# Seven unread matmuls in two waits of TensorE, ahead of the output stage of a recurrence and soft-MoE kernel

## The chip, the cores and the metric

The kernel runs on one core of one Trainium2 chip. The core has a matrix engine (TensorE, in the profile PE, with its weight loads listed apart as PEld), VectorE (DVE), ScalarE (ACT), GpSimd (POOL) and SyncE (SP), which run their own instruction streams and wait for each other through semaphores, and 16 DMA engines that move data between the chip's memory and the core's buffers (SBUF). Matmul results go to PSUM, which has 8 banks. The metric is the device time of one execution in microseconds, lower is better.

## The reference

Two steps. First a gated recurrence over 4 sequences of 5056 tokens and 256 channels; then a mixture of experts with soft slots over all 20224 tokens, with 8 experts of 4 slots:

```python
f = lower_bound + (1 - lower_bound) * sigmoid(f_logit);  i = 1 - f
for t in range(S):
    h = f[:, t] * h + i[:, t] * x[:, t];  y[:, t] = h
x = y.reshape(B * S, D)                                  # 20224 x 256
logits = x @ phi                                         # 20224 x 32
d = softmax(logits, over tokens);  slot_input = d.T @ x  # 32 x 256
for e in range(8):                                       # 4 slots each, F = 1024
    slot_out[e] = relu(slot_input[e] @ w1[e]) @ w2[e]
out = softmax(logits, over slots) @ slot_out             # 20224 x 256
```

Nothing of the output can be computed before all tokens have been seen, since `slot_input` sums over all of them.

## The kernel before

The work has three stages, and the order of the instructions on each engine is written out by hand.

The first stage (to about 126 us) runs over 40 units of 512 tokens of one sequence: load `f_logit` and `x`, sigmoid on ScalarE, gating on GpSimd, transposes on TensorE, the scan on VectorE, logits and their exponentials. The exponentials stay in SBUF as `etall` (32 slots of each of the 4 sequences on the 128 partitions, 5056 tokens). The expert weights are loaded meanwhile by GpSimd's DMA queue (`load_w`); the last two w2 matrices reuse a tile of the input buffers and appear in the profile as `w_t`.

The second stage (to about 142 us) computes the 32 slot outputs: hidden layer (L619), transposes (L634), the first four experts' second layer (L655), row sums of the exponentials (`row_sums`, L393, with reciprocals on VectorE at L664, L677 and L678), and the last four experts' second layer (L667): for each of them 8 matmuls into the PSUM tile `so_ps`. The last two experts' matmuls wait for `w_t`; the last expert's weights come in three parts. Then VectorE scales the sum to `slot_out` (L680), and GpSimd makes a second form of it, `slot_bd` (L682).

`spin(dst, k, w)` (L150 to L153) issues k matmuls of w columns with expert 0's first weights on both sides; nobody reads what they write. The kernel has three calls of it: 6 of 256 columns each before and after the transformation of the slot inputs, and 8 of 128 columns behind the last L667 matmul.

The third stage writes the output, 20.7 MB, in blocks. `pieces(0, 0)` does the first 2048 tokens of sequence 0: 16 matmuls of 256 columns (L699) into eight PSUM tiles, scaled by VectorE (L689) and ScalarE (L693) in turn, and seven output DMAs (L721). Then come `couple(end, 0)` and `couple(end, 1)`, `rest()`, `whole(0, 1)` and the other couples: matmuls of 512 columns for two sequences at once (L749), scaled by VectorE (L754) and ScalarE (L760), two DMAs each (L763). All output DMAs are issued by SyncE. The PSUM tiles of the couples take the banks that `pieces` used, so TensorE's stream holds a separate wait instruction ahead of the first L749 matmul, until VectorE has read the last of `pieces`. A second such wait stands ahead of the first L667 matmul.

On the chip a matmul of bf16 values is two TensorE instructions, a weight load and the matmul. In the numbering of the change's description, the first output matmul (L699) is TensorE's instruction 2217; the wait ahead of the first L667 is then 2083, and the wait ahead of the first L749 is 2248.

Of the kernel before, what the change touches and what calls it, by code (L numbers as in the profile page):

```python
# [9 lines left out]
F32 = mybir.dt.float32  # L10
# [8 lines left out]
def kernel(  # L19
# [11 lines left out]
    B, S, D = x.shape  # L31
# [4 lines left out]
    P = 128  # L36
# [113 lines left out]
    def spin(dst, k, w):  # L150
        for _ in range(k):
            nc.tensor.matmul(dst[:, ds(0, w)], w1_sb[0][:, 0, :P], w1_sb[0][:, 0, :w],
                             start=True, stop=True, skip_group_check=True)  # L153
# [8 lines left out]
    with tc.tile_pool(name="sp2", bufs=3) as sp2, \  # L162
# [225 lines left out]
        def row_sums(i):  # L388

            t0, n_r = blocks[i]  # L390
            ew = etall[:, ds(t0, P * n_r)].rearrange("s (p r) -> s p r", r=n_r)
            for r in range(n_r):
                nc.tensor.matmul(sums[:, ds((t0 // P + r) * B, P)], ew[:, :, r], ones,  # L393
                                 start=True, stop=True, skip_group_check=True)
            if i == len(blocks) - 1:
                nc.tensor.matmul(rs_ps[:, n_grp * R - 1, ds(0, B // 2)],
                                 left.rearrange("s t u -> s (t u)"), pair_ones,
                                 start=True, stop=True, skip_group_check=True)
# [196 lines left out]
    with tc.tile_pool(name="ew", bufs=1) as ew, \  # L595
         tc.tile_pool(name="pm", bufs=2, space=PSUM) as pm, \
         tc.tile_pool(name="pbig", bufs=1, space=PSUM) as pbig:

        rep2 = rep.rearrange("p b s -> p (b s)")

        sin = ew.tile([P, DC, NS], BF16, name="sin")
        nc.vector.tensor_scalar_mul(sin[:, 0], sin_ps[:, 0], omlb[:, ds(0, 1)])
        nc.scalar.activation(sin[:, 1], sin_ps[:, 1], ACT.Copy, scale=omlb[:, ds(1, 1)])

        cs1 = ew.tile([P, 1], F32, name="cs1")
        nc.vector.tensor_reduce(cs1, csum, AX.X, ALU.add)


        Q = 4
        H = F // 2  # L610
        his = []
        for q in range(E // Q):
            hi = ew.tile([P, F], BF16, name=f"hi{q}")
            for k in range(2):
                hi_ps = (psu.tile([P, H], F32, name="hi_ps", tag="up") if q == 0 else
                         pbig.tile([P, H], F32, name="hi_ps", tag=f"hi_ps{k}"))
                for o in range(DC):
                    for j in range(Q):
                        nc.tensor.matmul(hi_ps[ds(j * NS, NS)], sin[:, o],  # L619
                                         w1_sb[q * Q + j][:, o, ds(k * H, H)],  # L620
                                         start=(o == 0), stop=(o == DC - 1),
                                         skip_group_check=True)
                if k == 0:
                    nc.scalar.activation(hi[:, ds(k * H, H)], hi_ps, ACT.Relu)
                else:
                    nc.vector.tensor_scalar_max(hi[:, ds(k * H, H)], hi_ps, 0.0)
            his.append(hi)
        cs_ps = pm.tile([P, 1], F32, name="cs_ps", tag="pm")
        rcs = ew.tile([P, 1], F32, name="rcs")
        for q in range(E // Q):  # L630
            ht_ps = psu.tile([P, FC, P], BF16, name="ht_ps", tag="up")
            hi_v = his[q].rearrange("p (c f) -> p f c", f=FC)
            for fc in range(FC):
                nc.tensor.transpose(ht_ps[:, fc], hi_v[:, fc], ident)  # L634
            if q == 0:
                nc.tensor.matmul(cs_ps, rep2, cs1, start=True, stop=True)
                src = ht_ps.rearrange("p f (j s) -> p f j s", s=NS)[:, :, :, ds(0, SPE)]
                src = bass.AP(tensor=src.tensor, offset=src.offset,
                              ap=[list(src.ap[0]), [P, FC], [NS + SPE, Q], [1, SPE]])
                dst = hid[:, :, :, ds(0, SPE)]  # L640
                dst = bass.AP(tensor=dst.tensor, offset=dst.offset,
                              ap=[list(dst.ap[0]), [Q * NS, FC], [NS + SPE, Q], [1, SPE]])
                nc.scalar.copy(dst, src)
                nc.vector.reciprocal(rcs, cs_ps)
                continue
            for j in range(Q):
                s0 = (Q + j) * SPE
                src = ht_ps[:, :, ds(j * NS + s0, SPE)]
                copy = nc.scalar.copy if j % 2 == 0 else nc.vector.tensor_copy
                copy(wide[:, :, j, :, ds(s0, SPE)],  # L650
                     src.unsqueeze(2).broadcast_to([P, FC, B, SPE]))
        so4_ps = pm.tile([P, D], F32, name="so4_ps", tag="pm")
        for e in range(Q):
            for fc in range(FC):
                nc.tensor.matmul(so4_ps[ds(fc % 4 * NS, NS), :], hid[:, fc, e],  # L655
                                 w2_sb[e][:, fc],
                                 start=(e == 0 and fc < 4),
                                 stop=(e == Q - 1 and fc >= FC - 4),
                                 skip_group_check=True)
        so4 = ew.tile([P, D], F32, name="so4")  # L660
        nc.vector.tensor_copy(so4, so4_ps)
        so_ps = pm.tile([P, D], F32, name="so_ps", tag="pm")
        row_sums(0)
        nc.vector.reciprocal(rrow[:, :wide_r], rs_ps[:, :wide_r])  # L664
        for j in range(Q):
            for fc in range(FC):
                nc.tensor.matmul(so_ps, wide[:, fc, j].rearrange("p b s -> p (b s)"),  # L667
                                 w2_sb[Q + j][:, fc], start=j == 0 and fc == 0,
                                 stop=j == Q - 1 and fc == FC - 1, skip_group_check=True)
            if j == 0:  # L670
                nc.tensor.matmul(so_ps, rep2, so4, start=False, stop=False,
                                 skip_group_check=True)
                row_sums(1)
            if j == 1:
                row_sums(2)
                q = n_grp * R - 1
                nc.vector.reciprocal(rrow[:, wide_r:q], rs_ps[:, wide_r:q])  # L677
                nc.vector.reciprocal(rrow[:, q, ds(0, B // 2)], rs_ps[:, q, ds(0, B // 2)])  # L678
        spin(tail[:, 1], 8, P)
        nc.vector.tensor_scalar_mul(slot_out, so_ps, rcs)  # L680
        for u in range(2):
            nc.gpsimd.tensor_scalar_mul(slot_bd[:, u], slot_out, parity[:, ds(u, 1)])  # L682
# [138 lines left out]
```

## Time and profile before

| | us |
|---|---|
| median of 3 runs (199.0 to 199.07) | 199.04 |
| profiled execution, its own time | 198.93 |
| its span, first to last instruction | 197.2 |
| TensorE busy / VectorE / ScalarE / GpSimd | 150.5 / 142.1 / 138.2 / 103.2 |
| last weight part (`w_t`) landed | 142.04 |
| first output matmul (L699) started | 143.04 |
| first couple's matmul (L749) started | 146.42 |
| last L749 matmul ended | 175.55 |

The granted TensorE clock is 0.86 in the mean: 1.00 for most of the time to 145.46 us, 0.50 from there on. The DMA engines moved 70.75 MB in 14161 packets.

Times inside the profile are microseconds from the start of the span. Idle time on an engine that ends nothing costs nothing, so the profile is read from the last event backwards: what did the end wait for, and what did that wait for in turn.

### The profile page before, as it was taken

Reading aid. Unit: us, or ns where it says so; the run is one execution under the profiler, and the core shown is the slowest. Engines: PE = TensorE matmul, PEld = TensorE weight load, DVE = VectorE, ACT = ScalarE, POOL = GpSimd, SP = SyncE. Lnnn points to the kernel's source line nnn. Section 1 sums busy time; section 2 is a strip of 40 time slices with the busy share of each in tenths; the row PEclk is TensorE's granted clock in tenths of the full one; section 3 lists DMA queues with packets and bytes.
Section 4 is the critical chain, followed back from the end, with each engine's and each line's share of the span. In section 5 each row is a group of like instructions: output and inputs, shape, how many; then the busy total and the mean of one; then the engine's idle time right before and its main releaser. Section 6 shows DMA issues by size and latency. Waiting matters only on the chain.

```text
span 197.2 us, 3212 instructions
## 1 busy us (share of the span) xinstructions
PE 150.5 (76%) x1188; PEld 105.2 (53%) x1188; DVE 142.1 (72%) x163; ACT 138.2 (70%) x193; POOL 103.2 (52%) x78
## 2 busy tenths in 40 slices
PE   0688598897999979897988888998669999960000
PEld 0476467675766858665776676667443643410000
DVE  2669779989799999999999999332268878840000
ACT  3588678799799998999898797240058889990000
POOL 2589577874998488894969986290030000000000
PEclk9999789999999999999999999999975555555555
DMA  6999999999999999999999999999658999999995
GB/s 210 418 419 421 430 427 422 425 427 352 384 430 420 391 352 422 430 409 307 407 422 374 257 217 214 214 213 213 117 219 345 422 450 429 422 425 425 429 425 216
DMA packets 14161, 70.75 MB, mean 359 GB/s; under 512 B 1585, under 2 KB 2866, under 8 KB 10178
## 3 DMA queue, kind: packets, MB, share of 16 engines
q1 hardware_dynamic: 11520, 62.13, 76.2%
q0 software_dynamic: 2624, 8.42, 21.4%
q8 instruction: 9, 0.15, 0.3%
q14 instruction: 6, 0.05, 0.1%
q10 hardware_dynamic: 2, 0.00, 0.0%
HBM read 58.23 MB, written 20.71 MB: 400 GB/s over the span
## 4 chain that ended last, share of the span: by engine, by line
DMA 36%; PE 29%; DVE 13%; POOL 4%; issue 4%; ACT 3%; ACTq 0%; SPq 0%; DVEq 0%; POOLq 0%
DMA x_t<-in_x_dram 14%; PE op L749 12%; DVE h L313 9%; DMA w_sb<-in_moe_w_dram 7%; DMA w_t<-in_moe_w_dram 7%; DMA f_t<-in_f_logit_dram 7%; POOL u_t L246 4%; PE hp L326 4%; PE up L267 3%; PE sp L261 3%; DVE ht L345 3%; PE op L699 2%; PE slot_ps L183 1%; PE lg L359 1%; DVE ob L689 1%
## 5 line engine op out<-in xcount | busy, mean ns | idle before, releaser
L246 POOL TENSOR_TENSOR u_t<-s_t,x_t 128x1024 bf16<-128x1024 bf16 (+1 forms) x39 | 82.4, 2128 | 22.1 <-ACT s_t L235 14.3
L313 DVE TENSOR_TENSOR_SCAN h<-a,h,up 128x512 bf16<-128x512 f32 (+1 forms) x72 | 86.8, 1252 | 4.4 <-PE up L267 1.7
L235 ACT ACTIVATE s_t<-f_t 128x2048 bf16<-128x2048 f32 (+2 forms) x23 | 38.3, 1668 | 6.3 <-DMA f_t<-in_f_logit_dram 6.0
L326 PE MATMUL hp<-ident_f,h 128*128 128x128 f32 (+1 forms) x160 | 29.3, 307 | 8.2 <-DVE ht L345 6.4
L326 PEld LDWEIGHTS hp<-ident_f,h 128*128 128x128 f32 (+1 forms) x160 | 23.2, 207 | 19.3 <-DVE ht L345 12.8
L261 PE MATMUL sp<-ident_f,s_t 128*128 128x128 f32 x144 | 22.3, 300 | 6.7 <-ACT s_t L235 4.5
L749 PE MATMUL op<-slot_bd,etall 64*128 64x512 bf16 x62 | 25.0, 621 | 1.6 <-DVE ob L689 1.4
L295 ACT ACTIVATE a<-sp,lbs 128x1024 f32<-128x1024 bf16 x24 | 25.5, 1116 | 0.6 <-PE sp L261 0.6
L760 ACT ACTIVATE oc<-op,rrow 128x256 f32<-128x256 f32 x60 | 22.8, 489 | 3.6 <-PE op L749 3.0
L754 DVE TENSOR_TENSOR oc<-op,rrow 128x1024 f32<-128x1024 f32 x16 | 19.3, 1221 | 6.1 <-PE op L749 6.1
L261 PEld LDWEIGHTS sp<-ident_f,s_t 128*128 128x128 f32 x144 | 18.0, 155 | 8.7 <-ACT s_t L235 5.3
L302 ACT ACTIVATE a<-sp,lbs 128x512 f32<-128x512 bf16 (+2 forms) x22 | 17.8, 858 | 4.7 <-PE sp L261 4.3
L267 PE MATMUL up<-ident_f,u_t 64*128 64x64 f32 x192 | 17.8, 230 | 2.2 <-POOL u_t L246 2.1
L749 PEld LDWEIGHTS <-etall 64*128 64x128 bf16 x62 | 9.0, 155 | 16.2 <-issue 12.5
L267 PEld LDWEIGHTS up<-ident_f,u_t 64*128 64x128 f32 x192 | 14.0, 138 | 6.2 <-POOL u_t L246 2.8
L183 PE MATMUL slot_ps<-rep,ident_f 128*128 128x256 f32 x52 | 16.4, 410 | 0.0
L345 ACT COPY ht<-hp 128x512 f32<-128x512 f32 (+1 forms) x20 | 11.7, 583 | 3.8 <-PE hp L326 3.7
L345 DVE COPY ht<-hp 128x512 f32<-128x512 f32 (+1 forms) x20 | 13.3, 667 | 0.8 <-PE hp L326 0.8
L693 ACT ACTIVATE ob<-op,rrow 128x256 f32<-128x256 f32 x15 | 5.8, 478 | 11.2 <-PE op L699 11.1
L313 DVE TENSOR_TENSOR_SCAN h<-a,up 128x512 bf16<-128x512 f32 x8 | 9.3, 1209 | 2.6 <-ACT a L302 1.7
L261 PE MATMUL up<-ident_f,u_t 128*128 128x128 f32 x48 | 9.4, 327 | 0.7 <-POOL u_t L246 0.7
L359 PE MATMUL lg<-h,phi 128*32 128x512 bf16 (+1 forms) x80 | 9.4, 389 | 0.3 <-ACT et L383 0.2
(109 smaller groups left out, 145.7 us busy)
## 6 DMA issues: line engine op xcount, KB each, us to landing
f_t<-in_f_logit_dram SPq DMA_DIRECT2D x12, 1024.0 KB, 12.3
x_t<-in_x_dram SPq DMA_DIRECT2D x12, 1024.0 KB, 11.5
out_dram<-oc SPq DMA_DIRECT2D x6, 2048.0 KB, 11.3
w_sb<-in_moe_w_dram POOLq DMA_DIRECT2D x14, 512.0 KB, 10.9
f_t<-in_f_logit_dram SPq DMA_DIRECT2D x12, 512.0 KB, 8.5
x_t<-in_x_dram SPq DMA_DIRECT2D x12, 512.0 KB, 9.9
out_dram<-oc SPq DMA_DIRECT2D x4, 896.0 KB, 5.9
out_dram<-ob SPq DMA_DIRECT2D x1, 2048.0 KB, 8.7
```

Source lines behind the costliest of these rows:

```text
L183: nc.tensor.matmul(slot_bank[:, 1], ident_f, wide_rep, start=False, stop=False, skip_group_check=True)
L235: nc.scalar.activation(s_t, f_t, ACT.Sigmoid, scale=-1.0)
L246: nc.gpsimd.tensor_tensor(uts[n][:, :r], s_t[:, :r], x_t[:, :r], ALU.mult)
L261: nc.tensor.transpose(ps[:, :, r], t[:, r], ident_f)
L267: nc.tensor.transpose(v[:, :, r], t(r)[k].bitcast(F32), ident_f[k, k])
L295: nc.scalar.activation(a, sp[:, :, :, :, o], ACT.Identity, scale=nomlb[:, ds(o, 1)], bias=1.0)
L313: nc.vector.tensor_tensor_scan(h[:, :T, o], decays[n // 2, o][:, n % 2, :T], up[:, :T, o], hs[number(g - 1, b)][:, ds(used(g - 1) - 1, 1), ...
L326: nc.tensor.transpose(hp[:n_p, r], hw[:, :n_p, r], ident_f)
L345: copy(hts[g][:n_p, b].rearrange("p r d -> p (r d)").bitcast(F32), hps.pop(n)[:n_p].rearrange("p r c -> p (r c)"))
L749: nc.tensor.matmul(op[:, i_r].rearrange("p u d -> p (u d)"), ew[:, :, r + i_r], slot_bd[ds(j * 2 * NS, 2 * NS)].rearrange("s u d -> s (u d)"),
L754: nc.vector.tensor_tensor(ob[:, :, ds(r, k)].rearrange("p u r d -> p r u d"), op[:, ds(0, k)], scale[:, ds(r, k)].unsqueeze(3).broadcast_t ...
L760: nc.scalar.activation(ob[:, u, r + i_r], op[:, i_r, u], ACT.Copy, scale=scale[:, r + i_r, ds(u, 1)])
```

## The change

Seven calls' worth of matmuls are added to TensorE's stream with the existing `spin`: three of 256 columns behind `row_sums(0)` and ahead of the first L667 matmul, four behind `row_sums(2)`. They write to a tile of their own, `unread`, which has the PSUM bank of an earlier tile (`hi_ps0`), and which nobody reads. Each is a weight load and a matmul, so that all later TensorE instructions have a number higher by 6 behind the first call, and by 14 behind the second. The wait ahead of the first L667 becomes 2089, the first output matmul 2231, and the wait ahead of the first L749 2262. The other engines' instructions and their order are the same, and so are the DMAs; semaphore values that count TensorE's matmuls are higher by up to seven. Lines behind the change move by 2 or 3.

```diff
         row_sums(0)
         nc.vector.reciprocal(rrow[:, :wide_r], rs_ps[:, :wide_r])
+        unread = pbig.tile([P, H], F32, name="unread", tag="hi_ps0")
+        spin(unread, 3, D)
         for j in range(Q):
             for fc in range(FC):
                 nc.tensor.matmul(so_ps, wide[:, fc, j].rearrange("p b s -> p (b s)"),
...
             if j == 1:
                 row_sums(2)
+                spin(unread, 4, D)
                 q = n_grp * R - 1
                 nc.vector.reciprocal(rrow[:, wide_r:q], rs_ps[:, wide_r:q])
```

## The prediction

> **What bounds the kernel now.** I read four views, from the end backwards. First SyncE's own waits, which say what the last instruction waited for:
>
> ```profile
> SPq L763 <- DVE oc L754: 17.8, 5, 4.9
> SPq L816 <- DMA out_dram<-oc: 17.3, 1, 17.3
> ```
>
> Columns: total us, times, longest us. The program ends on the landing of the last output transfer, 17.3 us after everything else of SyncE's. TensorE, VectorE and ScalarE are done at 177 us of 197.2. So what counts is when the 16 DMA engines get through 20.7 MB of output. Second, the chain of waits up to the first output:
>
> ```profile
> 127.48 14.56 DMA w_t<-in_moe_w_dram
> 142.08 0.39 PE so_ps L667 x2
> ...
> 143.46 2.83 DVE ob L689 x5
> 146.42 1.90 PE op L749 x4
> ```
>
> The last expert weights land at 142.04, and the output stage hangs on them. Third, stretches of the output stage (after the start and length come the engines' busy times, then the granted TensorE clock, the DMA engines' mean busy share and GB/s):
>
> ```profile
> 127.00:142.00 15.00, 12.78 (x168) 9.90 (x167) 4.08 (x12) 2.28 (x6) 5.91 (x7) 1.00 1.00 195
> 142.70:144.70 2.00, 1.87 (x19) 1.70 (x17) 1.52 (x4) 1.14 (x4) 1.54 (x2) 1.00 0.03 8
> 145.25:146.00 0.75, 0.00 (x0) 0.00 (x0) 0.75 (x2) 0.75 (x3) 0.00 (x0) 0.64 0.68 242
> 146.00:148.20 2.20, 1.78 (x5) 0.74 (x7) 0.93 (x2) 0.25 (x1) 0.00 (x0) 0.50 1.07 413
> 150.55:151.20 0.65, 0.65 (x3) 0.23 (x2) 0.65 (x1) 0.28 (x2) 0.00 (x0) 0.50 0.06 25
> 152.20:194.70 42.50, 23.34 (x66) 9.64 (x64) 18.99 (x17) 22.95 (x61) 0.00 (x0) 0.50 1.01 428
> ```
>
> The transfers are nearly idle until 144.7, full from 146 to 150.3, and full from 151.35 to the end. Between, at 150.55 to 151.20, the share is 0.06: one engine of sixteen works, fifteen wait for the first couple block. Fourth, the queues:
>
> ```profile
> q1 hardware_dynamic: 11520, 62.13, 76.2%
> q8 instruction: 9, 0.15, 0.3%
> ```
>
> Queue 8 fetched instructions nine times, 16384 B each. The packet records behind this view give the starts: 29.61, 49.45, 62.38, 76.58, 93.30, 107.51, 124.61, 134.88, 148.29 us. Numbered as in the change's words (first output matmul 2217), TensorE had by then started instructions 207, 509, 731, 993, 1259, 1497, 1764, 2087, 2258: on average (2258-207)/8 = 256.4 apart. So a fetch belongs to every 256th TensorE instruction, and the ninth falls into the saturated output stage. It lasts 1.02 us on one DMA engine. The same records show that engine late with the first block's output: its last packet of it ends at 152.16, fourteen others' at 150.3 to 150.5, the last other's at 150.91. The parts: six 2048-byte packets before the fetch took 145 instead of 84 ns (0.37), the fetch 1.02, the next two 441 and 254 instead of 159 (0.38); together 1.77. The idle stretch to 151.35 hides 0.9 of it; the rest stays to the end, where that engine lands last, at 195.49. Another lands at 195.18, the other fourteen at 194.73 to 194.89.
>
> **The change part by part.** The profiled execution took 198.93 us (span 197.2, 1.73 around it), 0.11 under the median of 199.04; gains are worked out inside it and taken off the median.
>
> Three unread matmuls stand behind the first row sums. One of this form starts 0.11 us after the one before (L152, 128x256: six in 0.82 us, 273 ns each). They fill 133.87 to about 134.4, where TensorE stood for 0.69 us until VectorE's reciprocal (L664) let L667 start at 134.73. That reciprocal waits for the row sums' last matmul, ahead of the three. What is left is 0.3 us, and behind it stands the wait for weights at 139.49; cost 0. If that cover were gone: 0.33 us. The first of them waits for an earlier matmul into its PSUM bank, done by 130.4.
>
> Four more stand behind row_sums(2): from 138.39, last end about 139.0. TensorE waited there until 139.49 for w_t, later parts landing up to 142.04; cost 0, or 0.44 with weights over 0.5 us earlier. No other engine's order changes, no DMA is added; semaphore counts only shift by 7.
>
> What moves: each later TensorE instruction has a number 14 higher, so the ninth fetch comes 14 instructions sooner. When, depends on a wait. TensorE's sequencer stops at waits of its own; the one ahead of the first L749 is number 2248, passed at 146.31 (VectorE's last ob), and becomes 2262. The number F that triggers the ninth fetch is bounded so:
> - The fetch came 1.98 us after that wait was passed. If F were 2248 or less, the sequencer could have reached it with the first outputs, 143.0 to 144.4, and the lag would be 3.9 us or more on idle engines. So F is at least 2249, and the lag from trigger to packet at most 1.98.
> - The sixth fetch (107.51) came 1.32 us after wait 1491 (106.19). With a lag over 1.32, its trigger lay at or before 1491, and F, 3x256 later, is at most 2259. The fourth (76.58, wait 985 at 75.41) says 2265 with a lag over 1.17.
> - A lag near 2 also fits the other fetches, with the sequencer some 20 instructions ahead of the matmul running.
>
> So F lies in 2249 to 2259 if the lag is 1.32 to 1.98, and then the wait, now 2262, no longer stands before it: the trigger falls among the first outputs, at 142.5 to 144.4, and the packet at about 144 to 146.4 instead of 148.29.
>
> The Trainium skill (Runtime: NRT & Kernel Launch, Instruction fetch mechanics) says that code comes in 16 KiB blocks of 256 instructions, fits the spacing above, and calls the cost of a boundary mostly hidden. By that rule the change would be worth nothing and the time 199.04; the packet rows show an engine that ends late, so I go by them.
>
> What the move is worth. Below: a fetch at 144.8 or later keeps its 1.77, less what is idle in 145.25 to 146.00 (share 0.68: 0.24). That engine would end the first block at 150.4+1.53 = 151.94 instead of 152.16: gain 0.2. Above: packet done before 144.8, nothing late; the last landing is then 195.18 (gain 0.31) or, if the second engine's delay (28 packets of 615 to 649 instead of 611 ns, between 160 and 180 us) is not there in other executions, 194.87 (gain 0.62). Between: a fetch that costs 0.9 or less in 144.4 to 146 is wholly hidden by the idle 150.4 to 151.35. The likeliest start is near 145, so mostly hidden: I take 0.45, midway between 0.31 and 0.62. Sum: 0 + 0 - 0.45, 199.04 - 0.45 = 198.6. Its own range is gains of 0.2 to 0.65: 198.4 to 198.84.
>
> **Rivals.**
> - *The fetch doesn't move* (the change does not do what its number suggests): the lag is under 1.3 us and F in 2263 to 2273, so that the wait still holds it back; 14 instructions are then at most some 0.3 us. For: engines without load could be quicker. Against: the slowed packets that belong to the fetch begin at 147.4, only 1.1 us after the wait. 199.04, within 0.15.
> - *Slower: the fetch meets the last weights.* If the sequencer looks 60 or more instructions ahead, it triggers while TensorE waits at 139.5 to 140; two us later the packet stands in front of weight packets (their last start at 141.7) on one engine. Price: the eighth fetch took 0.94 us, all of it on the chain into 142.04, so 199.04+0.94 less the 0.6 gained = 199.4. It decides from a trigger before 139.9, where TensorE is at number 2192 of the new count. Against: the ninth fetch's wait at 2248 would not matter then in the way seen, and 20 ahead fits all nine.
> - *The clock holds one window longer.* The granted clock fell from 1.00 to 0.50 at 145.46 in the records; four more matmuls in 138.4 to 139.0 might put that off. The first couple's matmuls (427 ns apart, as against 109 for half the columns at full clock) would come twice as fast, the couple up to 1.0 us sooner, and the idle 150.4 to 151.35 would shrink: 198.0 to 197.8. Against: the stretch in which it fell, 142 to 145.5, is untouched, and the clock was 1.00 all through 127 to 142 without them.
>
> **How the numbers follow.** A measurement tells about 0.2% (0.4 us) from no change. Fetch moves: 0.64, of which 0.44 gain over 0.4 us and 0.20 less. Doesn't move: 0.22, all but 0.04 (split evenly) within the bound. Meets the weights: 0.09, slower. Clock: 0.05, faster. Faster 0.44+0.02+0.05 = 0.51; same 0.20+0.18 = 0.38; slower 0.09+0.02 = 0.11. The range, 198.2 to 199.2, leaves out the clock's case, the weights' and the outer parts of the rest, about 0.16.
>
> **What would show it.** Right: the ninth packet of queue 8 starts before 146.4; no engine works alone in the idle stretch before the couple, and the last landings lie closer together; L667 still starts by its weights at 139.49 and 142.08, the first L699 at 143.04. Wrong: a fetch still at 148, weights landing after 142.1, a clock other than 0.50 from 145.5, or a late engine without a fetch on it, which would mean that I have blamed the wrong cause.

## The result and the profile after

The changed kernel took 198.74 us in the median of 15 runs (197.89 to 198.85), the kernel before 199.04 (198.76 to 199.6, 15 runs): a ratio of 0.997, 95% interval 0.9957 to 0.9982. The forecast was 198.6.

The stretches after, with the columns as before: length, the five engines' busy times, granted TensorE clock, mean busy share of the DMA engines, GB/s.

```profile
127.00:142.00 15.00, 13.67 (x176) 10.48 (x174) 4.17 (x12) 2.28 (x6) 5.90 (x7) 1.00 1.00 196
142.70:144.70 2.00, 1.87 (x20) 1.70 (x18) 1.52 (x4) 1.05 (x3) 1.45 (x2) 1.00 0.06 12
150.75:151.30 0.55, 0.55 (x2) 0.23 (x2) 0.55 (x1) 0.18 (x2) 0.00 (x0) 0.50 0.00 0
152.20:194.70 42.50, 23.41 (x67) 9.72 (x64) 19.08 (x17) 23.00 (x61) 0.00 (x0) 0.50 1.01 430
```

Two rows differ. Between the first block and the first couple the share is 0.00: the engine that worked alone there before (0.06) is done when the others are. And in 142.7 to 144.7, where nearly nothing moved, the share is up from 0.03 to 0.06: the ninth instruction fetch now lies there. The packet records have it at 143.30 instead of 148.29 us, 1.36 us long (a fetch of queue 14 at 144.00 overlaps it). The first block's last packets end at 150.55 to 150.69 on all sixteen engines, as against 152.16 on the late engine before.

The two waits of TensorE, with the new matmuls in them (start, length, what; in brackets the idle time left and what ended it):

```profile
133.97 0.49 PE L152 MATMUL unread<-w_sb 128*128 128x256 bf16 x3
134.81 1.03 PE L669 MATMUL so_ps<-w_sb,wide 128*128 128x256 bf16 x8 [0.35 <-DVE rrow L664]
...
138.44 0.60 PE L152 MATMUL unread<-w_sb 128*128 128x256 bf16 x4
139.57 0.60 PE L669 MATMUL so_ps<-w_t,wide 128*128 128x256 bf16 x4 [0.53 <-DMA w_t<-in_moe_w_dram]
```

Both waits are still ended by what ended them before. The end hangs on the same thing, too:

```profile
SPq L819 <- DMA out_dram<-oc: 17.1, 1, 17.1
SPq L766 <- DVE oc L757: 3.6, 1, 3.6
```

To compare executions whose first stages differ by some tenths, the table takes the time from the start of the first output matmul to the end of the last output packet (last column but one), with the start of the fetch (the ninth; in `e5_late` the tenth) and the moment from which the granted clock is 0.50. The rows below the second are the experiments that follow; each is one profiled execution. The last column is that execution's own time.

| run | first output no. | wait no. | first output, us | fetch, us | clock 0.50 from | to last packet | us |
|---|---|---|---|---|---|---|---|
| before | 2217 | 2248 | 143.04 | 148.29 | 145.46 | 52.45 | 198.93 |
| the change | 2231 | 2262 | 143.12 | 143.30 | 146.14 | 52.13 | 198.84 |
| before_again | 2217 | 2248 | 143.21 | 144.13 | 147.77 | 51.86 | 198.66 |
| e1_same_number | 2217 | 2248 | 142.98 | 143.90 | 147.83 | 51.92 | 198.47 |
| e2_early | 2231 | 2262 | 143.12 | 143.19 | 146.21 | 52.12 | 198.82 |
| e3_six | 2223 | 2254 | 143.12 | 148.60 | 147.75 | 52.99 | 199.59 |
| e5_late | 2413 | 2444 | 144.24 | 157.55 | 146.86 | 53.65 | 201.35 |
| e6_weights | 2287 | 2318 | 144.39 | 141.38 | 145.64 | 52.13 | 200.11 |
| e7_hold | 2231 | 2276 | 143.17 | 143.26 | 153.92 | 51.51 | 198.25 |
| e8_hold_only | 2217 | 2262 | 143.06 | 144.08 | 152.47 | 51.77 | 198.40 |
| e8_again | 2217 | 2262 | 143.06 | 144.04 | 150.85 | 51.82 | 198.46 |
| e8_third | 2217 | 2262 | 143.10 | 144.07 | 152.30 | 51.97 | 198.67 |
| e10_earlier | 2245 | 2290 | 143.02 | 143.16 | 153.63 | 51.51 | 198.12 |
| e11_minus14 | 2203 | 2234 | 143.84 | 149.19 | 146.47 | 52.65 | 199.93 |

### The profile page after: what moved, and what is told of

It reads as the page before. It is cut to its first block, busy times and chain, and to the rows that moved or that the text cites. A ratio compares the mean times of both kernels' runs of the same rounds, so it can differ in the third digit from the quotient of the medians.

```text
span 197.1 us, 3226 instructions
## 1 busy us (share of the span) xinstructions
PE 151.9 (77%) x1195; PEld 106.4 (54%) x1195; DVE 142.1 (72%) x163; ACT 138.1 (70%) x193; POOL 103.1 (52%) x78
## 4 chain that ended last, share of the span: by engine, by line
DMA 29%; PE 27%; DVE 17%; POOL 7%; ACT 5%; issue 4%; ACTq 0%; SPq 0%; DVEq 0%; POOLq 0%
DMA x_t<-in_x_dram 14%; DVE h L313 12%; PE op L752 12%; DMA w_sb<-in_moe_w_dram 7%; DMA w_t<-in_moe_w_dram 7%; POOL u_t L246 6%; PE hp L326 3%; PE up L267 3%; DVE ht L345 3%; PE sp L261 2%; PE op L702 2%; PE slot_ps L183 1%; PE lg L359 1%; DVE ob L692 1%; ACT oc L763 1%
```

## The experiments

The theory: the number of an instruction decides when the ninth fetch comes, and with a late fetch its DMA engine sets the end. The rivals: TensorE's work in the waits does it, through the clock; or a fetch outside the output stage is free wherever it lies.

### Number or work: e1_same_number and e2_early

The first keeps the seven matmuls and the old numbers; the second has the new numbers and nothing in the waits.

```diff
 e1_same_number, on the changed kernel
-        spin(tail[:, 1], 6, D)
+        spin(tail[:, 1], 2, D)
...
-        spin(slot_bank[:, 1], 6, D)
+        spin(slot_bank[:, 1], 3, D)
 e2_early, on the kernel before, in idle(), with pads = seven ones, then nothing
+            for _ in range(pads.pop() if pads else 0):
+                nc.tensor.matmul(slot_bank[:, 1, ds(0, 1)], ident, ident[:, :1],
+                                 start=False, stop=False, skip_group_check=True)
```

> The seven unread matmuls stand where the change has them, but seven of the twelve older unread matmuls around the slot inputs (lines 583 and 592) are left out, so that the first output matmul keeps number 2217 and the wait ahead of the first couple number 2248. If the number does it (my theory): the ninth instruction fetch starts near 148.3 us again, one DMA engine is alone at work between the first block and the couple, and the time is that of before, 199.04 within 0.2. If TensorE's added work in the waits does it (rival: the clock or the gap is what counts): the time of the change, 198.74 or less.

> The other way round: nothing in the two waits, but seven matmuls of one column, unread, spread over seven of the idle fillers of the first stage, so that the numbers are those of the change (first output 2231, wait 2262). If the number does it: the ninth fetch starts at about 143.3 us, and the time is 198.74 within 0.25. If the place of the matmuls does it: 199.04 or, with the seven costing something, up to 199.3.

Measured: e1_same_number 199.07 us (198.47 to 199.31; before in the same batch 199.15), ratio to before 0.9998, interval 0.9984 to 1.0011; e2_early 198.77 (198.01 to 198.86), 0.9977, 0.9964 to 0.9991. The two intervals nearly touch, but eight of the twelve runs of e1_same_number lie above the longest of e2_early. So the gain comes with the number and not with the matmuls in the waits. The profile of e2_early repeats that of the change in the stretch that matters:

```profile
150.75:151.30 0.55, 0.55 (x2) 0.22 (x2) 0.55 (x1) 0.19 (x2) 0.00 (x0) 0.50 0.00 0
```

But one half of the expectation for e1_same_number failed: in its profiled execution the fetch was not near 148.3 but at 143.90, with the wait still numbered 2248 and passed only at 146.3. That execution was also the fastest of its twelve. So an early fetch is possible with the old numbers, and a single profile does not show what the others do.

### The same program twice: before_again

> The kernel before once more, for its ninth fetch alone. The run with the first output at 2217 and seven matmuls moved had it at 143.9 us, and the times of before spread from 198.3 to 199.7, so the trigger may be so near to the wait that it falls now ahead of it, now behind. Late (148 to 149) with a time over 198.9, or early (143 to 146) with a time under 198.8, would both say so; early with a time over 199 would say that the fetch isn't what makes the difference.

The kernel before, unchanged, had its fetch at 144.13 in this execution, with a time of 198.66. So the fetch of one program is now early, now late. The short times of before_again and e1_same_number are not the fetch's alone, though: the clock, too, fell 2.3 us later in them (147.77 and 147.83) than in the first profile (145.46). The early executions have another mark, SyncE's second output DMA issue. The timeline of SyncE from 144.3 to 144.7 gives the first two issues together (start, length, what); first before, then before_again, then the change:

```profile
144.02 0.82 SPq L721 DMA_DIRECT2D out_dram<-ob  x2
```

```profile
144.18 1.50 SPq L721 DMA_DIRECT2D out_dram<-ob  x2
```

```profile
144.10 0.92 SPq L724 DMA_DIRECT2D out_dram<-ob  x2
```

With the late fetch the second issue took 0.42 us. With a fetch that ended at 145.29 it took 1.10 and was over at 145.69; in e1_same_number (fetch over at 145.11) 1.15, over at 145.51; with the change (fetch over at 144.66) 0.52, over at 145.02. In each the issue ends 0.36 to 0.40 us after the fetch. So a fetch at 144 is not free: it holds the second output DMA, and in before_again the first block's last packets end at 151.13 to 151.27 on the sixteen engines, instead of 150.55 to 150.69 with the change. The fetches that were over by 144.66 held that issue by 0.1 us at most. It is not every issue under every fetch that is held: in before_again the first issue took its 0.35 us with the fetch under way since 144.13, and in e3_six an issue of 0.33 us started at 149.65, within the fetch (148.60 to 149.89). That SyncE's issues in turn hold up the fetch is not shown; why it comes at 144 in some executions and at 148 in others, I could not settle.

### Part of the shift: e3_six

```diff
-        spin(unread, 4, D)
+        spin(unread, 0, D)
```

> Only the first three unread matmuls: 6 instructions, first output 2223, wait 2254. My bounds put the number that triggers the ninth fetch at 2249 to 2259. If it is 2254 or less, the fetch moves ahead of the wait (start near 143.5 to 144.5 us) and the time is 198.75; if it is 2255 or more, the fetch stays behind it (148.0 to 148.3) and the time is 199.04. A gain in proportion to the number (rival: each instruction moves the fetch by its own length) would be 6/14 of 0.3, 198.91.

Measured: 198.90 us (198.39 to 199.59), ratio 0.9991, 0.9976 to 1.0006. The profiled execution had the fetch at 148.60. The median is between the two cases, and the spread of 1.2 us is like that of before in the same batch (198.34 to 199.72) and not like the two heaps of the change, 0.96 us apart at most with nine of fifteen runs within 0.14. So six instructions do not move the fetch to the safe side in every execution, and the result doesn't decide for a step or a proportion.

This profile also shows what a late fetch costs when the clock falls late. The clock fell at 147.75 us, as in before_again (147.77) and e1_same_number (147.83). With their early fetches those two took 51.86 and 51.92 us from the first output to the last packet; e3_six took 52.99. The couple's output came sooner than in the first profile, so that no idle stretch was left ahead of it:

```profile
150.48:152.00 1.52, 1.52 (x5) 0.31 (x3) 1.04 (x2) 1.52 (x5) 0.00 (x0) 0.50 1.08 449
```

One engine's last packet ends at 196.12, those of the fifteen others at 194.03 to 194.35. Nothing hid its lateness, and the late fetch cost 1.1 us instead of 0.3.

### The suspected cost doubled: e5_late

```diff
 on the kernel before, with the loop of e2_early in idle()
+        pads = [(98 + i) // 21 for i in range(21)]
```

> Ninety-eight unread one-column matmuls spread over the idle fillers of the first stage: numbers up by 196, so that the trigger that was some 5 instructions behind the wait ahead of the first couple (as a tenth fetch, 256 further) is some 65 behind it. Theory: that fetch starts later, at 149 to 155 us counted from the same landing of the weights, so that none or little of its engine's 1.8 us is hidden by the idle stretch ahead of the first couple; against before, where 0.9 is hidden, the time measured from the landing of the weights is 0.5 to 0.9 us longer, and the whole 199.5 to 200.0 if the first stage is unchanged. Rival: the fetch's engine doesn't set the end: 199.04.

Measured: 201.30 us (200.98 to 201.38), ratio 1.0113, 1.0098 to 1.0127. Of this, 1.20 us comes ahead of the output stage (first output matmul at 144.24 instead of 143.04), nearly all of it in the transfer of the last weights:

```profile
127.59 15.64 DMA w_t<-in_moe_w_dram
143.23 0.04 issue
```

It took 15.64 us instead of 14.56, with two fetches in it (129.89 and 137.73 us) instead of one (134.88). From the first output to the last packet it took 53.65 us, 1.20 more than before; I had expected 0.5 to 0.9. The fetch came at 157.55, in the full stretch. In its stretches the idle time ahead of the couple has no lone engine, and the end has one:

```profile
151.75:152.45 0.70, 0.70 (x4) 0.23 (x3) 0.70 (x1) 0.33 (x2) 0.00 (x0) 0.50 0.00 0
157.50:158.55 1.05, 1.05 (x3) 0.44 (x4) 1.05 (x2) 1.03 (x3) 0.00 (x0) 0.50 1.02 412
196.10:197.30 1.20, 0.00 (x0) 0.00 (x0) 0.00 (x0) 0.00 (x0) 0.00 (x0) 0.50 0.06 27
```

The last row is the plainest evidence: for 1.2 us at the end a single engine (0.06 is one sixteenth) still writes output. Its last packet ends at 197.89; fourteen others' end between 195.91 and 196.1, one at 196.37. A fetch of 0.95 us that nothing hides so leaves its engine 1.8 us late, which agrees with the 1.77 us added up from packets in the prediction.

### Too early: e6_weights

The same loop, with 35 in place of 98.

> Thirty-five unread one-column matmuls spread over the idle fillers of the first stage, nothing in the two waits: first output 2287, so that the ninth fetch's trigger lies some 34 instructions ahead of the first output, among the last experts' matmuls. The theory: the fetch starts at 140 to 142 us, while the last weights are on the same DMA engines; if one engine's weight packets wait for it, the last weights land up to 0.95 us later and the time is 199.0 to 199.6; if that engine has no weight packets left, the time is that of the change, 198.74. The rival that any fetch outside the output stage is free says 198.74.

Measured: two heaps, five runs from 198.08 to 198.99 and five from 199.76 to 200.11, ratio 1.0005, interval 0.9982 to 1.0027 (two more runs, at 201.17 and 201.38, are not in these). In the profiled execution, of the upper heap, the fetch ran from 141.38 to 142.36, and the last packets of `w_t` came after it: the last ends at 142.59 instead of 141.72 before. The chain of waits has the weights' landing 1.35 us later than before:

```profile
127.48 15.91 DMA w_t<-in_moe_w_dram
143.39 0.04 issue
143.43 0.39 PE so_ps L671 x2
```

The first output matmul starts at 144.39 instead of 143.04; from there on it took 52.13 us, as with the change. So the slower rival of the prediction is real in this execution, where the first output has number 2287, and dearer than the 0.94 us it was priced at. As in e5_late, two fetches (135.49 and 141.38) lie in the transfer of the last weights; the twelve other executions in the table have one, and there it took 14.55 to 14.56 us. No execution of the lower heap was profiled, so that the fetch missed the weights there is likely, not shown. With the change the weights landed at 142.13: its fetch does not reach them.

### The clock: e7_hold

The change's times lie in two heaps: nine of fifteen from 198.71 to 198.85, six from 197.89 to 198.31. The lower six have mean granted clocks of 0.849, 0.867 and 0.877, the upper nine 0.842 to 0.843 and 0.860 to 0.863. Each mean also holds what the clock did earlier in the execution, so this points to a later fall in the lower six without showing it. e2_early, which adds nothing in the waits, has such runs, too (198.01 and 198.21).

```diff
-        with tc.tile_pool(name="pfirst", bufs=8, space=PSUM) as pfirst:
+        with tc.tile_pool(name="pfirst", bufs=7, space=PSUM) as pfirst, \
+             tc.tile_pool(name="phold", bufs=1, space=PSUM) as phold:
             pieces(0, 0)
+            held_ps = phold.tile([P, 2 * D], F32, name="held_ps")
+            for _ in range(7):
+                nc.tensor.matmul(held_ps, etall[:, :P], etall[:, :2 * D],
+                                 start=True, stop=True, skip_group_check=True)
```

> The change, and seven more unread matmuls (512 columns, etall against itself) between the first block's matmuls and the wait ahead of the first couple, into a PSUM bank of their own (the first block has seven tiles instead of eight). The time of the change comes in two heaps, 198.75 and 197.9 to 198.3, and I hold that the lower one has a clock that falls a window later. If so, a TensorE kept busy in 144.9 to 146.3 makes the granted clock fall behind 148.5 in every run, the first couple's output starts up to 0.9 us sooner, and the median is 198.0. If the heaps have another cause: 198.74, or up to 199.0 with the bank missing.

Measured: 198.19 us (198.07 to 198.25, five runs), ratio to before 0.9961, 0.9949 to 0.9973. The clock fell at 153.92 in the profiled execution. The stretch of the first couple, in e7_hold and then in the changed kernel:

```profile
146.50:149.50 3.00, 2.53 (x11) 1.08 (x10) 1.94 (x2) 1.51 (x5) 0.00 (x0) 1.00 1.05 417
```

```profile
146.50:149.50 3.00, 2.99 (x9) 1.19 (x10) 1.44 (x2) 1.02 (x3) 0.00 (x0) 0.50 1.05 418
```

At clock 1.00 TensorE is busy for 2.53 us, and VectorE and ScalarE have done 1.94 and 1.51 us of couple work instead of 1.44 and 1.02. The couple's first packet starts at 150.83 instead of 151.43, right behind the first block's last (150.73): the idle stretch is nearly gone. The upper heap is absent from the five runs. Against the change itself, the two intervals overlap, so a gain over it is likely from the heaps, not shown by the intervals. The fall of the clock was seen in one of the five executions; that it was late in the others is inferred from their times.

### The wait's number: e8_hold_only, e8_again, e8_third

The seven matmuls of e7_hold on the kernel before: the first output stays 2217, and the wait becomes 2262.

> The kernel before with the seven 512-column matmuls in front of the wait alone, nothing in the two waits for weights: first output 2217 as before, but the wait ahead of the first couple is number 2262 as with the change. If the distance between the trigger and that wait decides, the ninth fetch is early (143 to 145) and the time is that of the change with the clock held, 198.0. If the first output's number decides, the fetch stays late and its engine keeps the end at 198.9 or more whatever the clock does.

> The kernel with first output 2217 and the wait at 2262, once more for its ninth fetch. If that fetch is ever seen behind the wait (148 us) here, where fourteen more instructions stand ahead of the wait, the wait's number is not what decides; if it is early again, that stays open.

> The same kernel and question: a fetch at 148 us says that the wait's number doesn't decide, a fetch at 143 to 145 us leaves it open.

Measured: 198.77 us (198.34 to 199.11), ratio 0.9987, 0.9976 to 0.9997. All three profiled executions have the fetch at 144.04 to 144.08, and SyncE's second issue at 0.99 to 1.22 us. So with the clock held and fourteen more instructions ahead of the wait, the fetch was early in three of three, but 0.8 us later than with the change, and the time is 0.58 us above that of e7_hold. Neither case of the expectation came true as a whole. Three early executions leave open whether the wait's number matters: with the wait at 2248 it was early in two of three. What they do show is that fourteen instructions ahead of the wait alone don't bring the fetch to where the same fourteen ahead of the first output bring it.

### Further down and further up: e11_minus14 and e10_earlier

```diff
 e11_minus14, on the kernel before: the two lines of e1_same_number alone
 e10_earlier, on e7_hold
-        spin(unread, 3, D)
+        spin(unread, 5, D // 2)
...
-                spin(unread, 4, D)
+                spin(unread, 9, D // 2)
```

> The kernel before with seven of its twelve unread matmuls around the slot inputs left out, nothing added: first output 2203, wait 2234. Theory of a race (the fetch's request against SyncE's output DMAs, not against TensorE's wait): the request comes some 0.6 us later than in before, always behind the first output DMAs, so the fetch is at 148 us or later in all executions, and no time is under 198.8, median 199.1 to 199.4. If the fetch were as often early as in before, the times would spread from 198.3 again.

> The kernel with the clock held (seven 512-column matmuls ahead of the first couple), and fourteen unread matmuls of 128 columns in the two waits instead of seven of 256: first output 2245. The traces so far: a fetch that ends by 144.3 leaves SyncE's second output DMA issue at its 0.43 us, one that ends at 144.7 to 145.3 holds it until 0.4 us after. Theory: the fetch starts near 142.7, ends before the first output DMA, and the time is 198.0 to 198.2, at or a little under the 198.19 with first output 2231. If the fetch meets the last weights as at 141.4: over 198.6.

e11_minus14: 198.99 us (198.80 to 199.93), ratio 1.0001, 0.9993 to 1.0010, no run under 198.80, fetch at 149.19 in the one profiled; the expected median was 199.1 to 199.4. The lone engine is back in the idle stretch:

```profile
151.35:152.05 0.70, 0.70 (x4) 0.23 (x3) 0.70 (x1) 0.33 (x2) 0.00 (x0) 0.50 0.06 23
```

In that batch, though, before itself had no run under 198.81 among 23, so the two don't differ and the expectation that before would be early more often than this kernel is not borne out by times. e10_earlier: 198.26 (ten runs from 197.93 to 198.35, two at 199.67 and 199.69), ratio 0.9973, 0.9956 to 0.9990. Fourteen more instructions moved the fetch only from 143.26 to 143.16 us, not to 142.7: between 2231 and 2245 the fetch hardly follows the number. It is no better than e7_hold, and the cause of the two runs near 199.7 is open.

## Why the prediction was right, point by point

- **What sets the end.** Right. The ninth fetch makes its DMA engine late, and that engine sets the end: shown by e5_late and e3_six from the dear side and by the change and e2_early from the cheap one. (Of the six slowed packets ahead of the fetch the first took 128 ns and not 145, which takes 0.02 us off the 1.77.)
- **The seven matmuls cost nothing.** Right. They left 0.35 and 0.53 us of the waits; the forecasts were 0.3 and 0.5.
- **The fetch moves ahead of the outputs.** Right in effect, at 143.30 us, earlier than the 144 to 146.4 stated. Since the reason given failed (next point), this was in part luck.
- **Why it moves.** Not upheld. The prediction bounded the trigger to numbers 2249 to 2259, so that the wait 2248 would always stand before it. The step that failed is the first bound, "F is at least 2249": the same program had the fetch at 144.13 and e1_same_number at 143.90, both more than 2 us before the wait was passed. In those it was asked for before the wait was passed, so the late fetch of the first profile may also have been asked for in time and held up for some 4 us, a lag I had ruled out because the engines were idle. What the runs put in its place: counted in the traces from the first output matmul on, TensorE was at number 2234 to 2236 when the early fetch started, in all eight executions with the first output at 2217 or 2231 that had it early. With 2231 that is 0.07 to 0.18 us after the first output, with 2217 it is 0.92 to 1.02 us, where the fetch meets SyncE's first output DMAs. So the change moves that number into a stretch in which the DMA engines are nearly idle (143.12 to 144); the three profiles with 2231 all have the fetch early. What makes it late in some executions with lower numbers stays open.
- **What the move is worth.** The mechanism was right, the size high: 0.45 taken, 0.30 measured in the medians. The mis-sized term is the choice between 0.31 and 0.62. The second engine's delay, which I took to be half there, is there in full in the profile of the change: one engine's last packet lands at 195.25, the others' from 194.81 to 194.96. Profile against profile the gain is 52.45 - 52.13 = 0.32 us from the first output on. That pair has the clock at 0.50 ahead of the first couple in both. The price is not one number: where the clock falls at 147.8 a late fetch costs 1.1 us (e3_six). And before is itself a mixture of early and late fetches and of early and late falls of the clock, which I had not expected, so the 0.30 between the medians need not be the 0.32 between the two profiles.
- **The rivals.** "Does not move" and "meets the weights" did not come about here; e6_weights shows the second to be real. The clock fell 0.68 us later in the profiled execution (146.14), while TensorE stood waiting until 146.51, which is not the rival's case. Six of the fifteen runs of the change lie at 197.89 to 198.31, about where that rival put the time; that the clock fell later in them is likely, not shown. The four added matmuls are not needed for it, since it fell at 147.77 in the kernel before.
- **The signs of being wrong.** Two of those listed came by little: the weights landed at 142.13 (limit 142.1), because their transfer started 0.10 us later and took as long as before, and the clock was not 0.50 from 145.5 but from 146.14. Neither bears on the fetch.
- **The rule that a block boundary is mostly hidden** (Trainium skill, Runtime: NRT & Kernel Launch, Instruction fetch mechanics) would have given 199.04. Measured: the place of the ninth fetch is worth 0.3 us in the median, and a fetch that nothing hides costs its DMA engine 1.8 us (e5_late, e3_six). A second fetch among the last weights went with a landing 1.08 us (e5_late) and 1.35 us (e6_weights) later; the other fetches were not priced. The measurement decides.

## What to carry to other kernels

Here an instruction fetch took up a DMA engine like any other transfer. When a stage is bound by DMA, see where the fetches of the longest instruction stream fall, and move one out of the saturated stretch with a few cheap instructions in a wait, placing it neither on the last loads nor on the first stores. A share of 0.06 between two full stretches is one engine of sixteen; ask what made it late and whether it is still late at the end. One profile shows one execution: where times of one program spread more than those of another, take a second one before naming a cause.

## What was not expected of the hardware

- The same program has the same fetch at 144.13 in one execution and at 148.29 us in another.
- An instruction fetch under way can hold SyncE's DMA issue: the second one took 0.99 to 1.22 us instead of 0.42, ending 0.36 to 0.44 us after the fetch (before_again, e1_same_number and the three executions of the e8 kernel). The first one was not held.
- The granted clock fell to 0.50 and stayed there though TensorE was busy for 2.99 of 3.00 us from 146.5 to 149.5 with matmuls on 64 rows. It fell at 145.46 to 147.83 us without the holding matmuls, differently from execution to execution, and at 150.85 to 153.92 with them. In all fourteen traces each stretch between two changes of the clock lasts a whole multiple of 3.41 us (119.47 is 35 of them in before).
